# Pooled keys by transposing transfers and VectorE instead of TensorE, from the third batch on

## The chip, the cores and the metric

The kernel runs on one core of a Trainium2 chip. The metric is the device time of one execution in microseconds (us), lower is better. The engines of the core run side by side and wait for one another through semaphores: TensorE (PE in the profile, its weight loads PEld), VectorE (DVE), ScalarE (ACT), GpSimd (POOL) and SyncE (SP), which here only issues transfers.

## The reference

Attention with pooled keys and values (8 batches, 8 heads, 576 tokens, 64 wide), then a token-mixing and channel-mixing block on x of 8 batches, 576 tokens, 512 wide:

```python
def _attn_ref(q, k, v):
    k_p = k.reshape(B, H, 72, 8, D).mean(axis=3)
    v_p = v.reshape(B, H, 72, 8, D).mean(axis=3)
    scores = scale * np.matmul(q, k_p.transpose(0, 1, 3, 2))
    scores = scores - np.max(scores, axis=-1, keepdims=True)
    attn = np.exp(scores)
    attn = attn / (np.sum(attn, axis=-1, keepdims=True) + 1e-09)
    return np.matmul(attn, v_p)

def _moe_ref(x, alpha1, beta1, w_tok, alpha2, beta2, w_ch1, w_ch2, lam):
    a1 = alpha1 * x + beta1
    tok = np.einsum('ts,bsd->btd', w_tok, a1)
    u = x + lam * tok
    a2 = alpha2 * u + beta2
    ch = np.maximum(a2 @ w_ch1, 0.0) @ w_ch2
    return u + lam * ch
```

So every eight neighbouring tokens of k give one pooled key, and each query is compared with 72 of them.

## The kernel before

The work runs in nine blocks of 512 tokens (block n has four chunks of 128 tokens). Beside the MLP of block n (mlp_A, then mlp_B or from block 2 on the seven products of product, with their sums in hidden_sum and gather) the kernel does the attention and token mixing of batch b = n + 1. Block 0 does batch 1; batch 0 comes ahead of the loop. The order on every engine is written by hand: each block makes a list of (time, step) pairs, sorts it by the times (numbers of about 0 to 32, not microseconds) and calls the steps in that order. An engine executes its instructions in the order of these calls, and SP and GpSimd issue their transfers in that order too. Steps near 29 of one block and near 0 of the next are neighbours.

k of a batch is handled in two halves u of four heads. load_k reads four tokens of each head per partition in float32. sum_k, on GpSimd, adds the four tokens, and writes the sum twice, side by side, in bfloat16 (k_bf, 128 partitions x 4 heads x 2 x 64; L373 and L375). att_K, on TensorE, makes pooled, transposed keys of it: for each head one matmul with k_bf as stationary operand and pool_main as moving one (L633; pool_main holds 0.125 where two partitions belong to one pooled token, 64 columns), and two more matmuls for the last 64 tokens of the heads (L639, from rem_k with pool_rem). The result ps_kp (128 x 288) goes from PSUM to kp_pool[u] by a cast (L645; VectorE, for batch 2 ScalarE). The last tokens ("rem", 512 to 575) of q and k are loaded by load_rem, and cast and added by cast_rem on GpSimd; for batches from 3 on a one-element memset of VectorE ahead of it (behind) sets when it may begin. att_Frem turns the q part by a transposing transfer on SP (L609), att_F turns q itself (L585), mix_uT turns the mixed tokens u_bf (L849).

att_S4(b, u) makes the scores: matmuls of kp with qT (L701) and with rem_qT (L708), and exp on ScalarE (L730) follows. att_V pools v on VectorE in three steps (L671), att_AV multiplies (L744, L748) and VectorE scales the result (L750, L752). load_v sends v of the next batch from SP; its buffer is free when att_V has read it. load_q_bf sends q from GpSimd, with a cast from float32 to bfloat16.

The listed times that matter: in the blocks of batches 3 to 7 sum_k stands at -0.9 and 0.3, load_q_bf of the next batch at 0.4 and 0.5, the first half of att_V at 0.2, 1.4 and 2.2, load_v of the next batch at 3.5 and 7.5, att_K at 4.1 and 6.1, hidden_sum 3 at 4.6, the second half of att_V from 5.0, att_S4 at 6.3 and 13.6. The stores of the block before stand at its 27.2 and 29.2, after att_Frem (26.72). In batch 2's block att_K stands at 2.9 and 4.9; its sum_k is done a block ahead.

wt_bf holds w_tok until it is transposed at the start; weight_sum later takes its place for T1, a sum of weights.

Of the kernel before, what the change touches and what calls it, by code (L numbers as in the profile page):

```python
# [7 lines left out]
FP = mybir.dt.float32  # L8
F16 = mybir.dt.float16
BF = mybir.dt.bfloat16  # L10
AF = mybir.ActivationFunctionType
ALU = mybir.AluOpType
AX = mybir.AxisListType

P = 128
# [195 lines left out]
def kernel(  # L211
# [18 lines left out]
    nc = tc.nc  # L230
    fast = ctx.enter_context(ExitStack())
    fast.enter_context(tc.manual_schedule())
    B, H, S, D = q.shape

    const = fast.enter_context(tc.tile_pool(name="const", bufs=1))
    work = fast.enter_context(tc.tile_pool(name="work", bufs=1))
# [16 lines left out]
    st1 = {}  # L253
# [97 lines left out]

    def cast_rem(b, eng, copy=None, behind=None):
        raw = st1[b]["rem_raw"]
        rq = work.tile([P, 2, 2, D], BF, tag="rem_q", bufs=2, name="rem_q")
        if behind is not None:
            behind.memset(rq[:, 0, 0, 0:1], 0.0)
        rk = work.tile([P, 2, 2 if b else 3, D], BF, tag="rem_k", bufs=2, name="rem_k")
        (copy or eng.tensor_copy)(out=rq.rearrange("p c h d -> p h c d"), in_=raw[:, 0])
        twice = [raw[:, 1, :, c].unsqueeze(2).to_broadcast((P, 2, 2, D)) for c in range(2)]
        if b:  # L360
            eng.tensor_tensor(out=rk, in0=twice[0], in1=twice[1], op=ALU.add)
        st1[b]["rem"] = rq, rk

    def cast_rem_k(eng):
        raw, rk = st1[0]["rem_raw"], st1[0]["rem"][1]
        eng.tensor_copy(out=rk[:, :, 0:2], in_=raw[:, 1])
        eng.tensor_copy(out=rk[:, :, 2], in_=raw[:, 1, :, 0])
# [11 lines left out]
    wt_bf = const.tile([P, 5 * S + 64], BF, tag="wt_bf", name="wt_bf")  # L379
# [65 lines left out]
    vp1_pool, kpT_pool, kp_pool, ET_pool = [], [], [], []  # L445
    for i in range(4):
        if i < 2:
            t = const.tile([SPG, 4, 66], F16, tag=f"vp1_{i}", name=f"vp1_{i}")
            nc.vector.memset(t, 8.0)
            vp1_pool.append(t)  # L450
            t = const.tile([P, 2, 4, SPG], BF, tag=f"kpT_{i}", name=f"kpT_{i}")
# [3 lines left out]
    for i in range(2):  # L455
        t = const.tile([SPG, 4, S + 64], F16, tag=f"ET_{i}", name=f"ET_{i}")
# [147 lines left out]
    def att_Frem(b, copy=None):  # L604

        st = st1[b]
        st["rem_qT"] = work.tile([P, 2, P], BF, tag="rem_qT", bufs=2, name="rem_qT")
        if copy is None:
            nc.sync.dma_start_transpose(out=st["rem_qT"],  # L609
                                        in_=st["rem"][0].rearrange("p c h d -> p (c h d)"))  # L610
            return
        ps_q = gp("ps_qr").bitcast(BF)
        for c in range(2):
            nc.tensor.transpose(out=ps_q[:, 128 * c:128 * c + 128],
                                in_=st["rem"][0][:, c].rearrange("p h d -> p (h d)"),
                                identity=identity_bf)
        copy(out=st["rem_qT"], in_=ps_q[:, 0:256].rearrange("p (c t) -> p c t", c=2))

    def double_k(u):

        nc.vector.tensor_copy(out=st1[0]["k"][u][:, :, 4], in_=st1[0]["k"][u][:, :, 0])
        if u == 0:
            cast_rem_k(nc.vector)

    def att_K(b, u, copy):

# [63 lines left out]
    def att_S4(b, u):  # L690

        st = st1[b]
        qT, kp, rest = st["qT"][u], kp_pool[u], st["rem_qT"]
        lo = [psB.tile([P, DM], FP, tag="ch", bufs=2, name="ps_s") for _ in range(2)]
        hi = [gp("ps_s") for _ in range(2)]
        r = [gp("ps_r")[0:SPG, 0:128].rearrange("p (h i) -> p h i", i=64) for _ in range(2)]

        def main(i):
            for a in range(2):
                rows = slice(64 * a, 64 * a + 64)  # L700
                nc.tensor.matmul(  # L701
                    out=(hi if i > 1 else lo)[a][0:SPG, 256 * (i % 2):256 * (i % 2) + 256],
                    lhsT=kp[rows, i, :], rhs=qT[rows, 2 * i:2 * i + 2, :])

        def rests(i):
            for a in range(2):
                rows = slice(64 * a, 64 * a + 64)
                nc.tensor.matmul(  # L708
                    out=r[a][:, i // 2], lhsT=kp[rows, i + a, :],
                    rhs=rest[rows, :, 2 * u + i // 2::4].rearrange("p c i -> p i c"))  # L710

        pairs = ((lo, 0), (hi, 2)) if u else ((hi, 2), (lo, 0))
        main(pairs[0][1])
        rests(pairs[0][1])
        main(pairs[0][1] + 1)
        main(pairs[1][1])
        rests(pairs[1][1])
        main(pairs[1][1] + 1)
        ET = ET_pool[u]
        for i in range(4):  # L720
            st["ET"][4 * u + i] = ET[:, i]

        def exp(k):
            if k < 2:
                o, i = ET[:, k::2, 512:S], r[k]
            else:
                a, (pair, h) = k % 2, pairs[k // 2 - 1]
                o = ET[:, h:h + 2, 256 * a:256 * a + 256]
                i = pair[a][0:SPG, :].rearrange("p (h i) -> p h i", i=256)
            nc.scalar.activation(out=o, in_=i, func=AF.Exp, bias=0.0, scale=0.125)  # L730

        st["exp", u] = exp

# [40 lines left out]

    def good_sums():

        lo = work.tile([P, H * B * 5], FP, tag="u_bf", bufs=4, name="good")
        hi = work.tile([P, H * B * 5], FP, tag="u_bf", bufs=4, name="good")
        every = recs.rearrange("p h b c -> p (h b c)")
        g = nc.gpsimd  # L780
        g.tensor_scalar(out=lo, in0=every, scalar1=MIN_REC, scalar2=None, op0=ALU.is_gt)
        g.tensor_scalar(out=hi, in0=every, scalar1=MAX_REC, scalar2=None, op0=ALU.is_lt)
        g.tensor_tensor(out=lo, in0=lo, in1=hi, op=ALU.mult)
        n = H * B * 5
        while n % 2 == 0:
            n //= 2
            g.tensor_tensor(out=lo[:, 0:n], in0=lo[:, 0:n], in1=lo[:, n:2 * n], op=ALU.add)
        for i in range(1, n):
            g.tensor_tensor(out=lo[:, 0:1], in0=lo[:, 0:1], in1=lo[:, i:i + 1], op=ALU.add)
        line = work.tile([1, P], FP, tag="u_bf", bufs=4, name="good_line")  # L790
        g.dma_start(out=line, in_=lo[:, 0:1])
        n = P
        while n > 1:
            n //= 2
            g.tensor_tensor(out=line[:, 0:n], in0=line[:, 0:n], in1=line[:, n:2 * n], op=ALU.add)
        g.tensor_scalar(out=flag, in0=line[:, 0:1], scalar1=P * H * B * 5 - 0.5, scalar2=None,
                        op0=ALU.is_lt)
# [127 lines left out]
    HALF = DM // 2  # L925
    wino = {}
# [4 lines left out]
    def weight_sum(i, g):  # L931
        lo, hi = w2[g], w2[g + 2]
        if not wino:
            wino["T1"] = const.tile([P, 8, HALF], BF, tag="wt_bf", name="w2_t1")
            both = const.tile([P, 6 * DM], BF, tag="vecs", name="w2_t3")
            wino["T3"] = both[:, 0:2048].rearrange("p (j d) -> p j d", d=HALF)
            spare = both[:, 2048:3072].rearrange("p (j t) -> p j t", t=HALF)
            wino["T2"] = [work.tile([P, 4, HALF], BF, tag="q_bf", bufs=4, name="w2_t2")
                          for _ in range(2)]
            wino["S2"] = [const.tile([P, 4, HALF], BF, tag=tag, name="h_s")  # L940
                          for tag in ("early", "al2_bc")]
            wino["S3"] = [const.tile([P, 4, HALF], BF, tag="lam_bc", name="h_s"), spare]
        T1, T2, T3, T4 = (wino["T1"][:, 4 * g:4 * g + 4], wino["T2"][g],
                          wino["T3"][:, 4 * g:4 * g + 4], lo[:, :, HALF:])
        o, a, b = {
            1: (T1, lo[:, :, HALF:], lo[:, :, 0:HALF]),
            3: (T3, hi[:, :, HALF:], lo[:, :, HALF:]),
            2: (T2, hi[:, :, HALF:], T1),
            4: (T4, hi[:, :, 0:HALF], T2),
        }[i]  # L950
        nc.vector.tensor_tensor(out=o, in0=a, in1=b, op=ALU.subtract)
# [150 lines left out]
    def attention(b):  # L1102


        first = b == 1
# [15 lines left out]
        for u in range(2):  # L1121
            if b != 2:
                todo.append((3.6 + 0.1 * u if first else -0.9 + 1.2 * u,
                             lambda u=u: sum_k(b, u, nc.gpsimd)))
            if first:
                todo.append((19.1 + 0.1 * u, lambda u=u: sum_k(2, u, nc.gpsimd)))
            todo.append((7.0 + 2.3 * u if first else (2.9 if b == 2 else 4.1) + 2.0 * u,
                         lambda u=u: att_K(b, u, nc.scalar.copy if b == 2 else nc.vector.tensor_copy)))
        for u in range(2):
            at = (9.0 if first else 6.3, 13.6)[u]  # L1130
            todo.append((at, lambda u=u: att_S4(b, u)))
# [144 lines left out]
```

## Time and profile before

| | us |
|---|---|
| three runs | 334.39, 339.01, 338.86 |
| their median | 338.86 |
| the profiled execution | 334.72 |
| span in its profile | 333.2 |

The profile is of one execution, and its numbers are to be held against 334.72. The span is cut into 40 equal slices in its second part; each digit is the busy share of an engine in tenths, the DMA row that of the core's 16 DMA engines:

```profile
## 2 busy tenths in 40 slices
PE   7999999999999999999999999999999999999994
...
DVE  6773376999579969776967797878687783363263
...
PEclk9999999999999999999999999999999999999999
DMA  7999979965894982499449933994340034003003
```

The clock granted to TensorE is full everywhere. The DMA row has a rhythm of one block (about 34 us, four slices): one or two full slices, then quieter ones.

In the rows of time that follow, the first number is the start in us from the beginning of the span, the second the duration; then come the engine, the line of the kernel, the operation, out<-in by the program's names, shapes, the count of merged instructions, and in brackets the idle time ahead with what ended it. For SP the duration is that of issuing. When a transfer has landed is told by completion events: each transfer raises a semaphore, and the last increment of it marks the landing.

### The profile page before, as it was taken

What the parts mean: (1) busy time and instruction counts of PE and PEld (TensorE: products, weight loads), DVE (VectorE), ACT (ScalarE), POOL (GpSimd) and SP (SyncE); (2) the same over time, 40 slices, a digit from 0 to 9 for tenths busy, and PEclk for the clock granted to TensorE, in tenths of its full rate; (3) what the DMA queues carried; (4) which work ended last, traced back from release to release, by engine and by line L of the source; (5) the groups of instructions that cost most, each with busy time, mean ns of one, the idle gap of its engine ahead of it and who ended that gap; (6) DMA issues with size and microseconds to landing.
All of it is one profiled execution on the core that took longest, in us unless ns stands there. A gap on an engine that the chain in (4) does not pass through costs nothing.

```text
span 333.2 us, 6535 instructions
## 1 busy us (share of the span) xinstructions
PE 325.3 (98%) x2524; PEld 209.2 (63%) x2524; DVE 233.1 (70%) x473; ACT 176.1 (53%) x324; POOL 117.8 (35%) x142
## 2 busy tenths in 40 slices
PE   7999999999999999999999999999999999999994
PEld 2667754455444576656775677557755765586583
DVE  6773376999579969776967797878687783363263
ACT  3776999368422861388128802781278235704700
POOL 8769535996247010800280027102610225100000
PEclk9999999999999999999999999999999999999999
DMA  7999979965894982499449933994340034003003
GB/s 113 197 205 278 280 153 268 161 175 124 169 264 69 226 175 80 91 233 164 138 120 215 173 117 90 218 184 151 65 136 2 0 65 143 4 0 128 0 31 96
DMA packets 66203, 45.83 MB, mean 138 GB/s; under 512 B 34381, under 2 KB 56533, under 8 KB 66170
## 3 DMA queue, kind: packets, MB, share of 16 engines
q1 hardware_dynamic: 51788, 32.60, 40.9%
q0 software_dynamic: 13856, 12.40, 22.2%
q10 hardware_dynamic: 526, 0.40, 0.5%
q8 instruction: 20, 0.33, 0.4%
q14 instruction: 13, 0.11, 0.1%
HBM read 38.30 MB, written 9.44 MB: 143 GB/s over the span
## 4 chain that ended last, share of the span: by engine, by line
PE 92%; DVE 4%; DMA 2%; issue 1%; ACT 0%; DVEq 0%; POOLq 0%
PE ps_h L878 35%; PE ps_w L994 26%; PE ps_tok L830 12%; PE ps_ch L898 8%; PE ps_av L744 2%; PE ps_s L701 2%; DVE v_u L671 2%; DMA q_bf<-in_q_dram 2%; PE ps_kp L633 1%; PE ps_q L590 1%; DVE x_tm L752 1%; PE ps_r L708 1%; PE ps_av L748 1%; PE ps_sc L681 0%; PE ps_warm L821 0%
## 5 line engine op out<-in xcount | busy, mean ns | idle before, releaser
L878 PE MATMUL ps_h<-u_fm,w 128*128 128x512 bf16 (+2 forms) x608 | 133.9, 369 | 0.8 <-DVE x_tm L752 0.3
L885 ACT ACTIVATE H<-ps_h,bias_cols 128x512 bf16<-128x512 f32 x144 | 98.2, 688 | 56.5 <-PE ps_h L878 55.4
L878 PEld LDWEIGHTS <-w 128*128 128x128 bf16 x608 | 65.7, 114 | 50.3 <-issue 2.6
L994 PEld LDWEIGHTS <-H 128*128 128x128 bf16 x560 | 53.5, 98 | 10.8 <-DVE u_sb L1012 1.2
L838 ACT CAST u_bf<-u_sb 128x512 bf16<-128x512 f32 x32 | 19.8, 619 | 70.6 <-issue 41.2
L994 PE MATMUL ps_w<-w,H 128*128 128x256 bf16 x448 | 53.8, 273 | 0.0
L766 POOL TENSOR_TENSOR xs<-x_tm,lamal_bc 128x512 bf16<-128x512 f32 x12 | 15.2, 1267 | 107.2 <-DVE x_tm L752 107.0
L1012 DVE TENSOR_TENSOR u_sb<-u_sb,ps_w 128x512 f32<-128x512 f32 x54 | 36.4, 685 | 18.7 <-PE ps_w L994 18.2
L830 PE MATMUL ps_tok<-xs,wtT 128*128 128x512 bf16 (+3 forms) x200 | 44.9, 380 | 0.0
L834 DVE TENSOR_TENSOR u_sb<-x_tm,ps_tok 128x512 f32<-128x512 f32 (+1 forms) x40 | 27.4, 684 | 10.4 <-PE ps_tok L830 10.4
L752 DVE TENSOR_TENSOR x_tm<-ps_av,recs 128x320 f32<-128x320 f32 x64 | 31.5, 491 | 2.7
L730 ACT ACTIVATE ET<-ps_s 72x512 f16<-72x512 f32 x56 | 32.3, 592 | 0.0
L898 PE MATMUL ps_ch<-w,H 128*128 128x512 bf16 x128 | 30.4, 379 | 0.0
L830 PEld LDWEIGHTS <-wtT 128*128 128x128 bf16 (+3 forms) x200 | 17.4, 100 | 16.0 <-issue 1.1
L671 DVE TENSOR_TENSOR v_u<-v_u 72x1024 f32<-72x1024 f32 (+1 forms) x24 | 25.3, 1053 | 0.2
L750 DVE RECIPROCAL recs<-ps_av 128x5 f32<-128x5 f32 x64 | 12.1, 189 | 18.1 <-PE ps_av L748 17.7
L994 PE MATMUL ps_w<-w_t,h_s 128*128 128x256 bf16 x168 | 22.6, 272 | 0.0
L898 PEld LDWEIGHTS <-H 128*128 128x128 bf16 x128 | 12.0, 98 | 13.7 <-issue 0.4
L373 POOL TENSOR_TENSOR k_raw<-k_raw 128x512 f32<-128x512 f32 x14 | 18.7, 1337 | 3.1 <-DMA k_raw<-in_k_dram 3.1
L963 DVE TENSOR_TENSOR H<-H,H 128x1024 bf16<-128x1024 bf16 x14 | 9.7, 690 | 14.3 <-ACT H L885 14.2
L375 POOL TENSOR_TENSOR k_bf<-k_raw 128x512 bf16<-128x512 f32 x14 | 19.1, 1367 | 1.1
L994 PEld LDWEIGHTS <-h_s 128*128 128x128 bf16 x168 | 16.4, 98 | 4.1
(158 smaller groups left out, 370.5 us busy)
## 6 DMA issues: line engine op xcount, KB each, us to landing
out_dram<-u_sb SPq DMA_DIRECT2D x30, 256.0 KB
k_raw<-in_k_dram SPq DMA_DIRECT2D x12, 512.0 KB
v_u<-in_v_dram SPq DMA_DIRECT2D x12, 512.0 KB
q_bf<-in_q_dram POOLq DMA_DIRECT2D x16, 256.0 KB, 6.2
w<-in_moe_w_ch_dram POOLq DMA_DIRECT2D x6, 512.0 KB, 12.9
out_dram<-u_sb SPq DMA_DIRECT2D x10, 128.0 KB
w<-in_moe_w_ch_dram POOLq DMA_DIRECT2D x1, 1024.0 KB, 15.0
k_raw<-in_k_dram POOLq DMA_DIRECT2D x2, 512.0 KB, 16.9
```

Of the source, the lines that this page charges most:

```text
L375: eng.tensor_tensor(out=bf, in0=twice[0], in1=twice[1], op=ALU.add)
L671: nc.vector.tensor_tensor(out=out, in0=t[:, :, 0:width], in1=t[:, :, width:2 * width], op=ALU.add)
L730: nc.scalar.activation(out=o, in_=i, func=AF.Exp, bias=0.0, scale=0.125)
L752: nc.vector.tensor_tensor(out=x[:, 1 - odd:6 - odd, dd:dd + D], in0=av[:, :, 0:64], in1=rec.unsqueeze(2).to_broadcast((P, 5, D)), op=ALU.mult)
L830: nc.tensor.matmul(out=ps_tok[p0:p1], lhsT=wtT[0:kk, at, P * c:P * c + p1 - p0], rhs=xs_pool[i][0:kk, sc, :], start=(sc == 0), stop=(sc == 4))
L834: nc.vector.tensor_tensor(out=s["u"][p0:p1, :], in0=x[p0:p1, 1 + c if c < 4 else 5 - 5 * i, :], in1=ps_tok[p0:p1, 0:DM], op=ALU.add)
L838: nc.scalar.copy(out=s["u_bf"], in_=s["u"])
L878: nc.tensor.matmul(out=ps_h[:, t0:t1 + one], lhsT=w1_of(cc, j), rhs=rhs, start=(cc == 0), stop=(cc == 3))
L885: nc.scalar.activation(out=H4[n, j // 4][:, j % 4, :], in_=ps_h, func=AF.Relu, bias=bias_cols[:, j:j + 1], scale=1.0)
L898: nc.tensor.matmul(out=ps, lhsT=H_of(n, j)[:, 128 * m:128 * m + 128], rhs=w2[j // 4][:, j % 4, :], start=(j == 0), stop=(j == NJ - 1))
L994: nc.tensor.matmul(out=ps, lhsT=stat(j), rhs=moving(j), stop=(j == 7), start=(first and (pp == 0 or alone) and j == 0), skip_group_check=True)
L1012: nc.vector.tensor_tensor(out=o, in0=o, in1=banks[key, "both"], op=ALU.add)
```

## The change

For batches 2 to 7 att_K is no longer called. Two new steps take its place. turn_k sends k_bf of a half (128 x 512) through a transposing transfer on SP into a tile kT; there is one such tile for each half. pool_k, on VectorE, adds neighbouring columns of kT into kp_pool (the two partitions that the matmul summed are neighbouring columns now). For the last tokens cast_rem writes q and k side by side in one tile of 512 columns, att_Frem turns both in one transfer into late["rem"], and pool_k(b, 0) sums k's part, four by four, in two reductions for both halves, from which pool_k(b, 0) and pool_k(b, 1) copy their share. The factor 0.125 that pool_main held moves into the scale of the exponential. For batch 2 turn_k is listed at 28.3 of the block before, ahead of the transposes of q, and pool_k at 0.1 of its own; for later batches turn_k at 0.35 and 0.95, pool_k at 4.1 and 6.1. Four tiles change place: late["rem"] and T1 share one tile in wt_bf's place, and the tiles of good_sums take places of rem_raw and k_bf instead of u_bf.

```diff
--- before.py
+++ after.py
@@ -351,15 +351,21 @@
 
     def cast_rem(b, eng, copy=None, behind=None):
         raw = st1[b]["rem_raw"]
-        rq = work.tile([P, 2, 2, D], BF, tag="rem_q", bufs=2, name="rem_q")
+        if b > 1:
+            both = work.tile([P, 4, 2, D], BF, tag="rem_k", bufs=2, name="rem_qk")
+            rq, rk = both[:, 0:2], both[:, 2:4]
+        else:
+            rq = work.tile([P, 2, 2, D], BF, tag="rem_q", bufs=2, name="rem_q")
+            rk = work.tile([P, 2, 2 if b else 3, D], BF, tag="rem_k", bufs=2, name="rem_k")
         if behind is not None:
             behind.memset(rq[:, 0, 0, 0:1], 0.0)
-        rk = work.tile([P, 2, 2 if b else 3, D], BF, tag="rem_k", bufs=2, name="rem_k")
         (copy or eng.tensor_copy)(out=rq.rearrange("p c h d -> p h c d"), in_=raw[:, 0])
         twice = [raw[:, 1, :, c].unsqueeze(2).to_broadcast((P, 2, 2, D)) for c in range(2)]
         if b:
             eng.tensor_tensor(out=rk, in0=twice[0], in1=twice[1], op=ALU.add)
         st1[b]["rem"] = rq, rk
+        if b > 1:
+            st1[b]["rem_both"] = both
 
     def cast_rem_k(eng):
         raw, rk = st1[0]["rem_raw"], st1[0]["rem"][1]
@@ -604,11 +610,15 @@
     def att_Frem(b, copy=None):
 
         st = st1[b]
+        if copy is None:
+            if not late:
+                late["room"] = const.tile([P, 2560], BF, tag="wt_bf", name="late_room")
+                late["rem"] = late["room"][:, 2048:2560].rearrange("p (c t) -> p c t", c=4)
+            st["rem_qT"] = late["rem"][:, 0:2]
+            nc.sync.dma_start_transpose(out=late["rem"],
+                                        in_=st["rem_both"].rearrange("p c h d -> p (c h d)"))
+            return
         st["rem_qT"] = work.tile([P, 2, P], BF, tag="rem_qT", bufs=2, name="rem_qT")
-        if copy is None:
-            nc.sync.dma_start_transpose(out=st["rem_qT"],
-                                        in_=st["rem"][0].rearrange("p c h d -> p (c h d)"))
-            return
         ps_q = gp("ps_qr").bitcast(BF)
         for c in range(2):
             nc.tensor.transpose(out=ps_q[:, 128 * c:128 * c + 128],
@@ -621,6 +631,29 @@
         nc.vector.tensor_copy(out=st1[0]["k"][u][:, :, 4], in_=st1[0]["k"][u][:, :, 0])
         if u == 0:
             cast_rem_k(nc.vector)
+
+    late = {}
+    rest_sums = const.tile([P, 2, 4, 8], FP, tag="rest_sums", name="rest_sums")
+
+    def turn_k(b, u):
+
+        if ("k", u) not in late:
+            late["k", u] = const.tile([P, 4, P], BF, tag=f"kpT_{u}", name="kT")
+        nc.sync.dma_start_transpose(out=late["k", u],
+                                    in_=st1[b]["k"][u].rearrange("p h a d -> p (h a d)"))
+
+    def pool_k(b, u):
+
+        kT = late["k", u].rearrange("p h (g r) -> p h g r", r=2)
+        nc.vector.tensor_tensor(out=kp_pool[u][:, :, 0:64], in0=kT[:, :, :, 0], in1=kT[:, :, :, 1],
+                                op=ALU.add)
+        for hh in range(0 if u else 2):
+            nc.vector.tensor_reduce(
+                out=rest_sums[:, hh], op=ALU.add, axis=AX.X,
+                in_=late["rem"][:, 2 + hh].rearrange("p (g i a) -> p a g i", i=4, a=4))
+        nc.vector.tensor_copy(
+            out=kp_pool[u].rearrange("p (r h) g -> p h r g", h=2)[:, :, :, 64:72],
+            in_=rest_sums[:, :, 2 * u:2 * u + 2])
 
     def att_K(b, u, copy):
 
@@ -727,7 +760,8 @@
                 a, (pair, h) = k % 2, pairs[k // 2 - 1]
                 o = ET[:, h:h + 2, 256 * a:256 * a + 256]
                 i = pair[a][0:SPG, :].rearrange("p (h i) -> p h i", i=256)
-            nc.scalar.activation(out=o, in_=i, func=AF.Exp, bias=0.0, scale=0.125)
+            nc.scalar.activation(out=o, in_=i, func=AF.Exp, bias=0.0,
+                                 scale=0.125 if b < 2 else 0.125 * 0.125)
 
         st["exp", u] = exp
 
@@ -774,8 +808,8 @@
 
     def good_sums():
 
-        lo = work.tile([P, H * B * 5], FP, tag="u_bf", bufs=4, name="good")
-        hi = work.tile([P, H * B * 5], FP, tag="u_bf", bufs=4, name="good")
+        lo = work.tile([P, H * B * 5], FP, tag="rem_raw", bufs=2, name="good")
+        hi = work.tile([P, H * B * 5], FP, tag="rem_raw", bufs=2, name="good")
         every = recs.rearrange("p h b c -> p (h b c)")
         g = nc.gpsimd
         g.tensor_scalar(out=lo, in0=every, scalar1=MIN_REC, scalar2=None, op0=ALU.is_gt)
@@ -787,7 +821,7 @@
             g.tensor_tensor(out=lo[:, 0:n], in0=lo[:, 0:n], in1=lo[:, n:2 * n], op=ALU.add)
         for i in range(1, n):
             g.tensor_tensor(out=lo[:, 0:1], in0=lo[:, 0:1], in1=lo[:, i:i + 1], op=ALU.add)
-        line = work.tile([1, P], FP, tag="u_bf", bufs=4, name="good_line")
+        line = work.tile([1, P], FP, tag="k_bf", bufs=2, name="good_line")
         g.dma_start(out=line, in_=lo[:, 0:1])
         n = P
         while n > 1:
@@ -931,7 +965,7 @@
     def weight_sum(i, g):
         lo, hi = w2[g], w2[g + 2]
         if not wino:
-            wino["T1"] = const.tile([P, 8, HALF], BF, tag="wt_bf", name="w2_t1")
+            wino["T1"] = late["room"][:, 0:2048].rearrange("p (j d) -> p j d", d=HALF)
             both = const.tile([P, 6 * DM], BF, tag="vecs", name="w2_t3")
             wino["T3"] = both[:, 0:2048].rearrange("p (j d) -> p j d", d=HALF)
             spare = both[:, 2048:3072].rearrange("p (j t) -> p j t", t=HALF)
@@ -1124,8 +1158,13 @@
                              lambda u=u: sum_k(b, u, nc.gpsimd)))
             if first:
                 todo.append((19.1 + 0.1 * u, lambda u=u: sum_k(2, u, nc.gpsimd)))
-            todo.append((7.0 + 2.3 * u if first else (2.9 if b == 2 else 4.1) + 2.0 * u,
-                         lambda u=u: att_K(b, u, nc.scalar.copy if b == 2 else nc.vector.tensor_copy)))
+            if first:
+                todo.append((28.3 + 0.01 * u, lambda u=u: turn_k(2, u)))
+                todo.append((7.0 + 2.3 * u, lambda u=u: att_K(b, u, nc.vector.tensor_copy)))
+                continue
+            if b > 2:
+                todo.append((0.35 + 0.6 * u, lambda u=u: turn_k(b, u)))
+            todo.append((0.1 + 0.01 * u if b == 2 else 4.1 + 2.0 * u, lambda u=u: pool_k(b, u)))
         for u in range(2):
             at = (9.0 if first else 6.3, 13.6)[u]
             todo.append((at, lambda u=u: att_S4(b, u)))
```

## The prediction

> **What bounds the kernel now.** First the page: busy time, then the chain of work that ended last.
>
> ```profile
> PE 325.3 (98%) x2524; PEld 209.2 (63%) x2524; DVE 233.1 (70%) x473; ACT 176.1 (53%) x324; POOL 117.8 (35%) x142
> ...
> PE 92%; DVE 4%; DMA 2%; issue 1%; ACT 0%; DVEq 0%; POOLq 0%
> ```
>
> TensorE is busy for 325.3 of 333.2 us. Whatever makes it wait in the middle is added to the end; whatever leaves it is taken off. Start and end aside, the chain leaves PE for more than a moment only once, at 70.5 to 83.9 us (batch 2's attention), where it runs through VectorE.
>
> Then one steady block, that of batch 4 (block 3, from 139.3 us), in order of time on PE:
>
> ```profile
> 143.61 0.28 PE L633 MATMUL ps_kp<-pool_main,k_bf 128*128 128x64 bf16 x4
> 143.73 0.21 PE L639 MATMUL ps_kp<-pool_rem,rem_k 128*128 128x16 bf16 x2
> 143.78 1.90 PE L878 MATMUL ps_h<-u_fm,w 128*128 128x512 bf16 x8
> 145.52 0.28 PE L633 MATMUL ps_kp<-pool_main,k_bf 128*128 128x64 bf16 x4
> 145.63 0.20 PE L639 MATMUL ps_kp<-pool_rem,rem_k 128*128 128x16 bf16 x2
> 145.77 0.30 PE L701 MATMUL ps_s<-qT,kp 64*72 64x256 bf16 x2
> ```
>
> Durations overlap in the pipeline, so I count from start to start: six k matmuls hold PE for 143.78 - 143.61 = 0.17 us. The scores (L701) follow the second six directly: k must be ready by 145.77.
>
> The same stretch on SP's queue, through which every transposing transfer goes:
>
> ```profile
> 139.10 0.58 SPq L921 DMA_DIRECT2D out_dram<-u_sb  x1
> 139.73 0.58 SPq L917 DMA_DIRECT2D out_dram<-u_sb  x1
> 140.41 1.31 SPq L849 DMA_TRANSPOSE u_fm<-u_bf  x1
> 141.82 1.00 SPq L917 DMA_DIRECT2D out_dram<-u_sb  x2
> 143.12 5.69 SPq L348 DMA_DIRECT2D v_u<-in_v_dram  x4
> ```
>
> SP issues stores, a transpose, stores, then v. The durations are those of issuing alone. Last the DMA share, in a quiet stretch and in this one:
>
> ```profile
> 130.50:138.00 7.50, 7.50 (x60) 5.00 (x58) 6.09 (x12) 2.65 (x5) 4.79 (x5) 1.00 0.34 70
> 139.30:149.00 9.70, 9.70 (x66) 5.48 (x64) 7.79 (x12) 7.16 (x13) 1.57 (x3) 1.00 1.09 211
> ```
>
> The last two columns are DMA share and GB/s: 0.34 of the sixteen engines against all of them. At the block's start q_bf loads (GpSimd issues two at 139.32 and 140.12) and stores of the block before fill the engines. The trace's completion events (the last increment of each transfer's semaphore) show what that does to SP's queue. In the quiet stretch transposes of 128x512 land 2.4 us after their issue begins. In the busy one: store of 139.73 at 144.02, transpose of 140.41 at 147.54, stores of 141.82 and 142.41 at 148.07 and 148.81. They land in the order of issue, and the transpose's packets begin at 144.0, when the store ahead is through. So SP's queue is served in order, and a transpose waits for every store ahead.
>
> **The change part by part.** The profiled execution took 334.72 us; sums stand against that. The median is 338.86 (runs 334.39, 339.01, 338.86), so the profile is like the fastest run, and 1.2% under the median.
>
> *Removed from PE:* twelve matmuls for each of batches 2 to 7, two groups of 0.17 us: 0.34 x 6 = 2.0 us off the path.
>
> *VectorE:* pool_k(b,0) is one add, two reductions and a copy, pool_k(b,1) an add and a copy. None is in the trace. The add (128x256, bf16) is nearest to the last v sum, 0.42 us (72x256); the reduction has the same shape as L468, 0.27; the copy of 128x32 lies between a memset (0.06) and the reciprocal of 128x5 (0.18), I take 0.18. So pool_k(b,0) is 0.42 + 2 x 0.27 + 0.18 = 1.1 us and pool_k(b,1) 0.6, less two casts of 0.45 from batch 3 on (batch 2's were ScalarE's): +0.8 a block. From batch 3 on VectorE is busy 5.4 of the first 6.5 us of most blocks, so those 0.8 are hidden; only batch 2 pays.
>
> *SP's queue and the new wait.* turn_k(b,0) and (b,1) stand behind the previous block's last stores and ahead of v. Each holds SP for 1.2 to 1.3 us (the u_fm rows); v of batch b+1 goes out 2.5 us later, and is wanted a block later: nothing. GpSimd has k_bf ready (139.37 for batch 4) before SP comes to it (142.8). Now pool_k(b,0) makes VectorE wait for the landing. Behind it on VectorE stand a hidden sum (L963) and the second half of v's sums, and PE's scores wait for kp, with everything behind them. The stores ahead are unchanged, so turn_k lands after them. Its own packets take 0.6 us of all sixteen engines in the quiet stretch (512 packets of 256 bytes); beside q_bf loads the u_fm transposes took 2.2 and 3.5 us after the store ahead landed (batches 6 and 4). I take 0.6 where q_bf is through (or, in batch 3, nearly), 2.2 for batch 5, whose second q_bf lands at 184.10. kp is ready 1.1 us after that, and the loss is against the start of the scores in the profile, which holds the 0.34 already:
>
> - batch 3: last store 113.11, kT 113.7, kp 114.8, scores were at 110.85: +3.9
> - batch 4: 148.81, 149.4, 150.5; 145.77: +4.7
> - batch 5: 180.64, 182.8, 183.9; 179.39: +4.5
> - batch 6: 217.32, 217.9, 219.0; 214.30: +4.7
> - batch 7 (no q_bf loads beside it): 247.31, 247.9, 249.0; 247.92: +1.1
>
> *Batch 2* has no such crowd: its turn_k goes out behind the transpose of 68.41, from 69.7 and 71.0, and lands after 2.4 us, at 72.1 and 73.4. VectorE comes to pool_k at 71.9, so pool_k(2,0) ends at 73.2 and pool_k(2,1) at 74.0, and v's sums begin 2.2 us later than now (71.81). That is the stretch where PE already waits for VectorE: +2.2, with its 0.34 inside. qT lands at 75.1 instead of 72.45 and makes the scores 0.8 late (74.34), inside these 2.2.
>
> *The rest:* q and k's last tokens in one transfer add 256 columns to one with slack (rem_qT lands at 139.26, used at 145.90). The scale of the exponential is a constant. good_sums' tiles end a wait of GpSimd (L781, 9.6 us) on which nothing hangs. Nothing.
>
> Sum: 2.2 + 3.9 + 4.7 + 4.5 + 4.7 + 1.1 = 21.1; 334.72 + 21.1 = 355.8, say 356.
>
> Bounds: pool_k(b,0) at 0.7 (short copy, overlapped starts), turn_k at 0.6 everywhere, batch 2 at 1.5: 1.5 + 3.5 + 4.3 + 2.5 + 4.3 + 0.7 = 16.8. The other end: pool_k at 1.9, as VectorE's v sums beside GpSimd ran near twice as long (72x512: 1.36 against 0.68), turn_k at 2.2 in batch 3 and 3.5 in batch 5: 3.2 + 6.3 + 5.5 + 6.6 + 5.5 + 1.9 = 29.0.
>
> The Trainium skill, VectorE: DVE Perf Modes, "The three transpose paths", speaks against such a change: it lists 390 ns for a bf16 block of 128x128 on TensorE and 1309 ns by DMA. By an estimate from that page four blocks one after another would take 5.2 us, 2.8 more than the quiet row, and the sum 17 us more. The trace disagrees: four blocks land in 2.4 us from issue.
>
> **The rivals.** (A) *The transfers land in time.* If a transpose were not held by the stores ahead, it would land 2.4 us after issue. With issue right behind the stores (106.7, 142.9, 175.3, 211.7, 244.5) kp would come at 110.6 (VectorE is free for it at 109.5), 146.4, 178.8, 215.2, 248.0: against the scores -0.3 (the removed matmuls alone), +0.6, -0.3, +0.9, +0.1, and +2.2 for batch 2: +3, 338. With batch 2 covered too, only PE's 2.0 us are left: 332.7, faster than before. It decides where landing follows issue by less than about 2 us more than in the quiet stretch. For it: the quiet rows, 130 to 138 us. Against: the 7.1 us of the transpose of 140.41, one place ahead in the same queue. The Trainium skill, DMA: Bandwidth & Descriptors, "Rules for kernel authors", gives this rival as a rule: issue early, wait late, and the fixed setup cost is overlapped. The quiet transposes agree with it; the one of 140.41 does not.
>
> (B) *Part of it.* Landings are receipts, and packets of the next transfer may run before them; if turn_k came 2 us sooner each time, the stalls were 1.9 + 2.7 + 2.5 + 2.7 + 0, with batch 2 +12: 347.
>
> (C) *VectorE becomes the bound everywhere:* +0.8 in five blocks, +2.2, -1.7 for the matmuls of those five: +4.5, 339. Against: its idle time ahead of kp's cast is 0.9 us in the blocks of batches 4 to 7.
>
> **How the numbers follow.** Two per cent, 6.8 us, is about what a measurement of this kernel can tell from no change. Forecast 0.70, B 0.10 (both slower by over 2%), A 0.13 and C 0.03 (within), and 0.04 for a gain of over 2%, which the 2.0 us of PE can't give except through the spread of the runs. So 0.80, 0.16, 0.04. The range runs from below B to the upper bound on the scale of the median: (334.72 + 29.0) x 338.86 / 334.72 = 368; low 343 leaves out A and C.
>
> **What would show it.** In the changed profile: no L633 or L639 rows after 36 us; PE idle of 3 to 5 us ahead of the first scores of batches 3 to 6, released by VectorE; VectorE idle ahead of pool_k's add, released by the DMA of kT; kT landing behind the stores ahead of it. Wrong if kT lands within 3 us of issue in those blocks, or VectorE does not wait there; then A holds.

## The result and the profile after

The changed kernel takes 365.46 us (median of 4 runs, 363.39 to 366.04) against 338.91 (median of 4, 334.39 to 339.01): ratio 1.0813, 95% interval 1.0727 to 1.0898. It is slower, by more than the sum of the prediction but inside its range. The profiled execution took 365.94 us against 334.72, 31.2 us more.

The page of the changed kernel, first its busy times, then clock and DMA in 40 slices, then the chain that ended last by engine:

```profile
PE 330.6 (91%) x2421; PEld 210.2 (58%) x2452; DVE 237.7 (65%) x499; ACT 176.2 (48%) x322; POOL 117.2 (32%) x142
...
PEclk9999999999999899989999799989999999999999
DMA  8999949768889671798439691697435005203002
...
PE 74%; DMA 11%; DVE 9%; issue 2%; SPq 2%; POOL 0%; DVEq 0%; POOLq 0%
```

PE's share of the chain fell from 92 to 74%, and DMA and VectorE took over. The clock row, flat before, has four dips. Who waited for whom, over the whole span (us in total, times, longest):

```profile
DVE kp L648 <- DMA kT<-k_bf: 27.2, 6, 7.1
...
PE ps_s L734 <- DVE kp L654: 21.7, 5, 5.7
```

That is the wait of the prediction: VectorE waits for kT in all six batches, and PE waits for VectorE's kp ahead of five groups of scores. Batch 4's block again, SP's queue, then VectorE, then PE. The block starts 10.4 us later than before the change (149.7 instead of 139.3), so add that when comparing:

```profile
150.81 1.31 SPq L883 DMA_TRANSPOSE u_fm<-u_bf  x1
152.21 1.00 SPq L951 DMA_DIRECT2D out_dram<-u_sb  x2
153.31 4.00 SPq L642 DMA_TRANSPOSE kT<-k_bf  x2
```

```profile
153.05 0.42 DVE L704 TENSOR_TENSOR vp<-v_u 72x256 f16<-72x256 f32 x1
160.16 0.42 DVE L648 TENSOR_TENSOR kp<-kT 128x256 bf16<-128x256 bf16 x1 [6.68 <-DMA kT<-k_bf]
160.50 0.47 DVE L651 TENSOR_REDUCE rest_sums<-late_room 128x32 f32<-128x128 bf16 x2
161.00 0.18 DVE L654 CAST kp<-rest_sums 128x32 bf16<-128x32 f32 x1
```

```profile
149.68 6.21 PE L912 MATMUL ps_h<-u_fm,w 128*128 128x512 bf16 x27
161.24 0.43 PE L734 MATMUL ps_s<-qT,kp 64*72 64x256 bf16 x2 [5.36 <-DVE kp L654]
161.46 0.28 PE L741 MATMUL ps_r<-late_room,kp 64*72 64x64 bf16 x2
...
162.39 3.53 PE L912 MATMUL ps_h<-u_fm,w 128*128 128x512 bf16 x11
```

By the completion events the two stores issued at 152.21 and 152.79 land at 158.82 and 159.95, and kT, issued at 153.31, at 160.13: right behind them. VectorE takes it up at 160.16, kp is done at 161.18, PE starts at 161.24. The last row holds something the prediction did not have: eleven matmuls of 512 columns in 3.53 us, where twelve took 2.78 at the same place before the change:

```profile
146.48 2.78 PE L878 MATMUL ps_h<-u_fm,w 128*128 128x512 bf16 x12
```

Stretches of the changed kernel's execution (the column before the last two is the granted clock):

```profile
156.00:161.00 5.00, 0.00 (x0) 0.00 (x0) 0.81 (x3) 0.61 (x1) 0.00 (x0) 1.00 1.15 247
161.00:164.40 3.40, 3.16 (x17) 1.58 (x18) 3.35 (x7) 1.00 (x4) 0.00 (x0) 0.50 0.44 84
164.40:168.00 3.60, 3.55 (x25) 1.99 (x25) 2.75 (x7) 3.60 (x7) 0.00 (x0) 1.00 0.55 129
```

PE stands still for 5 us, and then works at half clock for 3.4. The trace's clock records show four such times in the middle: 3.41 us from 120.03, 3.41 from 160.99, 6.83 from 198.53, 3.41 from 242.91. The first begins 0.4 us after the stall of batch 3 has ended (119.65), the others within the stalls of batches 4, 5 and 6.

### The profile page after: what moved, and what is told of

The parts are those of the page before. It is cut to its first block, busy times and chain, and to the rows that moved or that the text cites. A ratio compares the mean times of both kernels' runs of the same rounds, so it can differ in the third digit from the quotient of the medians.

```text
span 364.0 us, 6390 instructions
## 1 busy us (share of the span) xinstructions
PE 330.6 (91%) x2421; PEld 210.2 (58%) x2452; DVE 237.7 (65%) x499; ACT 176.2 (48%) x322; POOL 117.2 (32%) x142
## 4 chain that ended last, share of the span: by engine, by line
PE 74%; DMA 11%; DVE 9%; issue 2%; SPq 2%; POOL 0%; DVEq 0%; POOLq 0%
PE ps_h L912 24%; PE ps_w L1028 24%; PE ps_tok L864 10%; DMA kT<-k_bf 10%; PE ps_ch L932 6%; PE ps_av L778 2%; PE ps_s L734 2%; DVE v_u L704 2%; DMA q_bf<-in_q_dram 1%; SPq L951 1%; DVE kp L648 1%; DVE w L963 1%; DVE u_sb L868 1%; DVE u_sb L1046 1%; PE ps_q L596 1%
## 5 line engine op out<-in xcount | busy, mean ns | idle before, releaser
L912 PEld LDWEIGHTS <-w 128*128 128x128 bf16 x608 | 66.7, 115 | 57.2 <-issue 10.1
L800 POOL TENSOR_TENSOR xs<-x_tm,lamal_bc 128x512 bf16<-128x512 f32 x12 | 15.2, 1268 | 133.6 <-DVE x_tm L786 133.4
L864 PE MATMUL ps_tok<-xs,wtT 128*128 128x512 bf16 (+2 forms) x193 | 44.5, 380 | 0.4
L734 PE MATMUL ps_s<-qT,kp 64*72 64x256 bf16 x112 | 12.9, 308 | 22.3 <-DVE kp L654 21.7
L864 PEld LDWEIGHTS <-wtT 128*128 128x128 bf16 (+3 forms) x200 | 17.4, 100 | 16.0 <-issue 1.1
L704 DVE TENSOR_TENSOR v_u<-v_u 72x1024 f32<-72x1024 f32 (+1 forms) x24 | 23.6, 984 | 0.2
L648 DVE TENSOR_TENSOR kp<-kT 128x256 bf16<-128x256 bf16 x12 | 5.8, 483 | 27.2 <-DMA kT<-k_bf 27.2
L734 PEld LDWEIGHTS <-kp 64*72 64x72 bf16 x112 | 6.7, 122 | 28.6 <-DVE kp L654 24.9
```

The costliest lines, as they stand in the source:

```text
L704: nc.vector.tensor_tensor(out=out, in0=t[:, :, 0:width], in1=t[:, :, width:2 * width], op=ALU.add)
L734: nc.tensor.matmul(out=(hi if i > 1 else lo)[a][0:SPG, 256 * (i % 2):256 * (i % 2) + 256], lhsT=kp[rows, i, :], rhs=qT[rows, 2 * i:2 * i + ...
L864: nc.tensor.matmul(out=ps_tok[p0:p1], lhsT=wtT[0:kk, at, P * c:P * c + p1 - p0], rhs=xs_pool[i][0:kk, sc, :], start=(sc == 0), stop=(sc == 4))
L912: nc.tensor.matmul(out=ps_h[:, t0:t1 + one], lhsT=w1_of(cc, j), rhs=rhs, start=(cc == 0), stop=(cc == 3))
```

## The experiments

Times of single executions differ by up to 3.8 us before any changed step runs (the last section has the numbers). So one number is given for all beside the time: the stretch from the first token-mixing matmul (L830 before, L864 after) to the last matmul, both by their starts in the trace. It is 328.33 - 21.60 = 306.7 us before the change and 358.93 - 24.11 = 334.8 in the changed kernel. Four single executions ran first, beside one of 335.54 of the kernel before on the same chip.

**Stores behind turn_k.** Only the order in SP's queue:

```diff
-        store(n, m)
+        if n == 0 or m < 2:
+            store(n, m)
...
-                for m in range(4):
+                for m in range(4 if n > 5 else 0):
...
+        if 2 <= n <= 6:
+            for m in range(2 if n == 2 else 0, 4):
+                todo.append((1.2 + 0.01 * m, lambda m=m: store(n - 1, m)))
```

> Only the order on SP's queue changes: in the blocks of batches 3 to 7 the stores of the block before (for batch 3 the last two of them) go out behind turn_k, not ahead. GpSimd's q_bf loads stay as they are. Theory (turn_k waits in its queue for the stores ahead of it): kT lands before VectorE comes to it in batches 3, 5 and 7, and at most 2 us late in batches 4 and 6, where one u_fm transpose stays ahead of it; the stalls of 4.4, 5.1, 5.5, 5.1 us ahead of the scores shrink to under 1 us in batches 3 and 5 and under 2.5 us in 4 and 6, the half clock after them goes, and the time is 336 to 343 us. Rival (a transpose is slow whenever q_bf loads run beside it, whatever stands ahead of it): the stalls stay over 3 us in batches 4 and 6, time over 352. Rival (VectorE's new work is what is late): nothing changes, 360 to 367.

Measured: 343.82 us, stretch 311.5. The waits, the same two rows:

```profile
DVE kp L648 <- DMA kT<-k_bf: 8.6, 4, 3.5
...
PE ps_s L734 <- DVE kp L654: 3.6, 2, 2.1
```

23 of the 28 us of the stretch are back. kT(3, 0), (5, 0) and (7, 0) land 2.4 to 2.5 us after issue. The new order does two things for them: no store is ahead any more, and (3, 0) and (5, 0) go out 1.6 and 1.0 us ahead of the first q_bf load (batch 7 has none). (4, 0) and (6, 0) go out 0.3 and 0.6 us behind that load, and land 7.0 and 5.9 us after issue. Only a u_fm transpose stands ahead of them, and it has landed at 146.07 and 217.26, 5.8 and 4.8 us before kT does. kT(5, 1) has nothing but kT(5, 0) ahead, and lands 5.7 us behind it. So a transpose beside q_bf loads is slow with no store ahead of it: in this the first rival was right. Its stalls of over 3 us did not come because turn_k now goes out 3.4 and 3.2 us earlier in these two blocks, counted from the token-mixing matmuls before them. Two stalls are left, the longest 2.1 us, and the clock stays full through them. The time is 0.8 us above the range expected because this execution's start took 3.8 us longer than that of the kernel before.

**q_bf loads out of the way.** The queue's order is the changed kernel's; the loads beside it go out later:

```diff
-                    at = {1: 14.0, 2: 6.5}.get(b, 0.4) + 0.1 * u
+                    at = {1: 14.0, 2: 6.5}.get(b, 6.2) + 0.01 * u
...
-                        b + 1, u, nc.vector if b == 2 else None)))
+                        b + 1, u, nc.vector if b >= 2 else None)))
```

> Only the q_bf loads move: in the blocks of batches 3 to 6 they wait for a memset of VectorE that stands behind pool_k, so they no longer run beside the stores and turn_k. The queue order on SP is that of the changed kernel. Theory (stores that share the DMA engines with q_bf loads are slow, and the queue passes their delay on to turn_k): the stores ahead land within 3 us of their issue, turn_k within 3.5 us, stalls under 1.5 us, time 337 to 344 us. Rival (the order in the queue alone, whatever the load): stalls over 3 us and 352 or more. Rival (VectorE's new work): 360 to 367.

Measured: 338.81 us, stretch 310.0.

```profile
DVE kp L648 <- DMA kT<-k_bf: 8.4, 5, 2.5
...
PE ps_s L734 <- DVE kp L654: 2.8, 3, 1.2
```

Now kT lands 2.4 to 2.6 us after issue for batches 3 to 6, though the same stores stand ahead of it, and the longest stall is 1.2 us. From issue to landing, in us, by completion events (in brackets how long after the first q_bf load kT was issued):

| | changed kernel | stores behind | q_bf out of the way |
|---|---|---|---|
| kT(3, 0) | 7.4 (2.2) | 2.5 (-1.6) | 2.5 |
| kT(4, 0) | 6.8 (3.6) | 7.0 (0.3) | 2.6 |
| kT(5, 0) | 8.4 (1.1) | 2.4 (-1.0) | 2.6 |
| kT(6, 0) | 6.7 (3.8) | 5.9 (0.6) | 2.6 |
| kT(7, 0), no q_bf load | 3.2 | 2.4 | 3.2 |

So the q_bf load is what makes kT late: without it the order costs 0.8 us at most (batch 7), and beside it kT is late with stores ahead or without. In the changed kernel the delay falls on the stores ahead, and the queue hands it on. The order counts because it decides whether turn_k goes out before the loads begin. How long kT would take at its place in the changed kernel, beside the loads but without the stores, was not tried. Either change removes over four fifths of the loss.

**PE kept busy in the stall.** Twenty matmuls with an unused result ahead of the scores:

```diff
+        if not u and 2 < b < 7:
+            busy = psB.tile([P, DM], FP, tag="ch", bufs=2, name="ps_busy")
+            for _ in range(20):
+                nc.tensor.matmul(out=busy, lhsT=w2[3][:, 0, 0:P], rhs=w2[3][:, 0])
```

> The changed kernel with twenty matmuls of 128x512 (about 4.3 us) whose result nobody uses ahead of the first scores of batches 3 to 6, so that PE waits at most about 1 us there. Theory (after the stalls PE runs at a granted clock of 0.5 for one or two periods of 3.41 us, which costs 1.3 to 1.6 us in each of four blocks): the granted clock stays 1.0 from the start-up to the tail, the scores begin when they did, and the time falls by 5 to 6.5 us to 357 to 361. Rival (the blocks lose that time because VectorE has a backlog after its wait): the time stays at 363 to 367.

Measured: 359.06 us, stretch 330.3; the clock records show no half clock between 10.47 us and the tail. Batch 4's block on PE:

```profile
151.47 4.48 PE L729 MATMUL ps_busy<-w 128*128 128x512 bf16 x20
158.88 0.30 PE L738 MATMUL ps_s<-qT,kp 64*72 64x256 bf16 x2 [2.92 <-DVE kp L654]
...
159.59 2.78 PE L916 MATMUL ps_h<-u_fm,w 128*128 128x512 bf16 x12
```

PE still waits, for 2.92 us, and the twelve matmuls behind take 2.78 us as before the change. The stretch fell by 4.5 us, not 5 to 6.5; 2.3 us of the fall in time are a shorter start. But the part that the clock owns can be read without the rest: from the first scores of a batch to the first token-mixing matmul of its block it is 15.83 us in all four batches before the change, 17.42, 17.22, 17.46 and 17.11 in the changed kernel, and 15.83 four times here. The half clock costs 1.59 + 1.39 + 1.63 + 1.28 = 5.9 us, and all of it goes. VectorE's backlog behind its wait, the rival, costs nothing that this shows. The missing 1.4 us lie ahead of the scores, which begin 1.9 and 0.6 us later in the blocks of batches 4 and 6 than in the changed kernel, and 0.4 and 0.8 earlier in those of 3 and 5: batch 4's kT lands 8.7 us after issue here, 6.8 there.

**Nobody waits.** kT and k's turned last tokens are sent and not read; the keys come from the old matmuls:

```diff
-                                 scale=0.125 if b < 2 else 0.125 * 0.125)
+                                 scale=0.125)
...
-            todo.append((0.1 + 0.01 * u if b == 2 else 4.1 + 2.0 * u, lambda u=u: pool_k(b, u)))
+            todo.append(((2.9 if b == 2 else 4.1) + 2.0 * u, lambda u=u: att_K(
+                b, u, nc.scalar.copy if b == 2 else nc.vector.tensor_copy)))
```

> The transfers of the changed kernel all go out (turn_k, the joint one of q and k), but kT and k's turned last tokens are never read: the pooled keys of batches 2 to 7 come from the matmuls of the kernel before, at their old places, with the old scale. Theory (the wait is what costs, not the traffic): 334 to 341 us, and no idle time of PE ahead of the scores in batches 3 to 7. Rival (twelve more transposes on SP's queue crowd out v, k, u_fm and the stores): 345 or more.

Measured: 336.85 us, stretch 306.8, that of the kernel before (306.7). kT lands late as in the changed kernel (7.8 us after issue in batches 4 and 5, 6.5 and 5.4 in 3 and 6), and PE goes on without a gap:

```profile
147.35 0.28 PE L666 MATMUL ps_kp<-pool_main,k_bf 128*128 128x64 bf16 x4
147.47 0.20 PE L672 MATMUL ps_kp<-pool_rem,rem_qk 128*128 128x16 bf16 x2
147.60 0.30 PE L734 MATMUL ps_s<-qT,kp 64*72 64x256 bf16 x2
```

The transfers, the joint one of q and k among them, cost nothing. The whole cost is with the reader: VectorE's wait for kT, and pool_k itself, which this run leaves out too. The next two runs part these.

**turn_k ahead of the stores, and the same with batch 2 left to TensorE.** Both were timed against the kernel before in five rounds. The first moves turn_k to the end of the block before:

```diff
-            if b != 2:
-                todo.append((3.6 + 0.1 * u if first else -0.9 + 1.2 * u,
-                             lambda u=u: sum_k(b, u, nc.gpsimd)))
+            if first:
+                todo.append((3.6 + 0.1 * u, lambda u=u: sum_k(b, u, nc.gpsimd)))
+            elif b < B - 1:
+                todo.append((23.2 + 0.1 * u, lambda u=u: sum_k(b + 1, u, nc.gpsimd)))
+                todo.append((27.0 + 0.01 * u, lambda u=u: turn_k(b + 1, u)))
...
-            if b > 2:
-                todo.append((0.35 + 0.6 * u, lambda u=u: turn_k(b, u)))
```

> The changed kernel with turn_k of batches 3 to 7 listed at 27.0 of the block before, right behind att_Frem and ahead of the stores and of the fifth u_fm transpose (sum_k is called earlier for that, at the same place in GpSimd's order). q_bf loads as in the changed kernel. Theory (only the place in the queue and the load beside it made turn_k late): kT lands 2.4 to 4 us after issue and ahead of VectorE in all five blocks, no stall ahead of their scores; each of the five blocks is 0.3 us shorter than before the change (the matmuls gone), batch 2's block still 1.9 longer. From the first token-mixing matmul to the last matmul 307 us (306.7 before the change, 334.8 in the changed kernel), time 333 to 340 by the start-up clock, ratio 0.99 to 1.01. Rival (matmuls removed gain nothing because other work of the block fills the time): 308.5 or more for that stretch.

Measured: 335.84 us (median of 12) against 335.9 (median of 23), ratio 1.000, interval 0.996 to 1.0039; stretch 307.1. SP's queue and PE in batch 4's block:

```profile
141.65 2.53 SPq L642 DMA_TRANSPOSE kT<-k_bf  x2
144.27 1.22 SPq L955 DMA_DIRECT2D out_dram<-u_sb  x2
```

```profile
144.84 4.05 PE L912 MATMUL ps_h<-u_fm,w 128*128 128x512 bf16 x18
148.81 0.30 PE L734 MATMUL ps_s<-qT,kp 64*72 64x256 bf16 x2
```

kT(b, 0) lands 2.4 to 2.5 us after issue in all five blocks; in those of batches 3 to 6 it goes out 0.7 to 1.4 us ahead of the first q_bf load. kT(b, 1), a place behind it, takes up to 6.4 us beside the q_bf loads, again with no store ahead, but is wanted later. The scores follow the MLP's matmuls with no gap, and the five blocks are 0.30 to 0.35 us shorter than before the change, as the removed matmuls said. Batch 2's block is still 2.0 us longer. The second version takes that away:

```diff
-                                 scale=0.125 if b < 2 else 0.125 * 0.125)
+                                 scale=0.125 if b < 3 else 0.125 * 0.125)
...
-                todo.append((28.3 + 0.01 * u, lambda u=u: turn_k(2, u)))
...
-            todo.append((0.1 + 0.01 * u if b == 2 else 4.1 + 2.0 * u, lambda u=u: pool_k(b, u)))
+            if b == 2:
+                todo.append((2.9 + 2.0 * u, lambda u=u: att_K(b, u, nc.scalar.copy)))
+            else:
+                todo.append((4.1 + 2.0 * u, lambda u=u: pool_k(b, u)))
```

> As the run before it, and batch 2's pooled keys by TensorE as before the change (no turn_k and pool_k there; its scale stays 0.125). Theory (batch 2's loss of 1.9 us is VectorE's, which has no idle time in that stretch, and five blocks gain 0.34 us each): from the first token-mixing matmul to the last matmul 305.0 us, 1.7 under the kernel before the change, ratio 0.990 to 1.000. Rival (batch 2's loss lies in the order of SP's queue around its block or the joint transfer of last tokens): 306.5 or more.

Measured: 334.12 us (median of 12), ratio 0.9943, interval 0.9915 to 0.9971; stretch 305.7. This beats both kernels, by about half a per cent of the one before: the interval leaves out 1, but the gain is less than the 2% that the prediction counts as a change. The stretch is between the theory's 305.0 and the rival's 306.5. Batch 2's block is 0.46 us longer than before the change; its profile has a wait of 1.33 us there that the kernel before doesn't show:

```profile
70.81 2.75 PE L912 MATMUL ps_h<-u_fm,w 128*128 128x512 bf16 x12 [1.33 <-DMA u_fm<-u_bf]
```

That u_fm transpose stands in SP's queue behind the joint transfer of the last tokens, which waited for GpSimd. The changed kernel has the same wait (1.34 us), and the execution in which nobody waits has 0.92 us and no loss in its block. The wait is not what costs: VectorE sets the length of this block, and is behind earlier. It starts the first product ahead of v's sums (L941; L907 before) 12.72 us after the block's first token-mixing matmul here and in the changed kernel, 12.27 before the change and 12.29 where nobody waits. The last v sum ends 26.30, 27.71, 25.84 and 25.88 us into the block in the same four executions, and the length of the block moves with it. The other runs that keep pool_k are as late at L941 (12.7 to 12.8). Why VectorE is behind there stays open.

## Why the prediction was right, and where its sum was short

It forecast slower, 356 us in a range of 343 to 368, and the time is 365.46. Between the two profiles, 31.2 us apart, the parts come out so (by the starts of the first scores and of the first token-mixing matmul in each block):

| part | predicted | measured |
|---|---|---|
| batch 2's block | +2.2 | +1.9 |
| stall of batch 3 | +3.9 | +4.4 |
| batch 4 | +4.7 | +5.1 |
| batch 5 | +4.5 | +5.5 |
| batch 6 | +4.7 | +5.1 |
| batch 7 | +1.1 | +0.2 |
| half clock behind four stalls | 0 | +5.9 |
| the start, before any changed step | 0 | +2.5 |
| the tail, and what lies around the span | 0 | +0.6 |
| sum | 21.1 | 31.2 |

*The number* is in the range partly by luck. The bounds of the sum end at +29.0, 363.7 us, and the two profiles are 31.2 apart; what brings 365.46 inside is the step from the profile to the median of three runs (363.7 to 368; 23 later executions of the kernel before have a median of 335.9), and not one of the terms that were missing.

*The wait.* Right in place and direction; the stalls of batches 3 to 6 came out 0.4 to 1.0 us longer than forecast. kT landed 0.2 to 0.5 us behind the last store ahead of it in batches 3, 4, 6 and 7 (0.6 was taken), 2.7 in batch 5 beside a q_bf load (2.2). The stores themselves were taken as unchanged. The last one ahead landed 0.4 to 0.8 us later within its block than before the change in batches 3 to 6, and 0.7 earlier in batch 7, which accounts for most of the differences. That a transpose waits for every store ahead fits these landings, but is half of the cause: with the q_bf loads moved and the order kept the delay is gone, and with the stores moved and the loads kept it stays wherever kT still goes out beside a load.

*Removed matmuls.* 0.34 us for each batch, confirmed by 0.30 to 0.35 where nothing waits.

*VectorE.* pool_k(4, 0) took 1.02 us from 160.16 (1.1 predicted). Batch 2's pool_k, beside GpSimd's work, took 3.6 us instead of 1.7:

```profile
75.16 1.20 DVE L648 TENSOR_TENSOR kp<-kT 128x256 bf16<-128x256 bf16 x1 [0.29 <-DMA kT<-k_bf]
...
77.67 1.13 DVE L654 CAST kp<-rest_sums 128x32 bf16<-128x32 f32 x1
78.71 2.79 DVE L704 TENSOR_TENSOR v_u<-v_u 72x1024 f32<-72x1024 f32 x2
```

It waited for kT only 0.3 us there, and the v sums behind ran faster than before, so that the block lost 1.9 us after all, of which 0.45 lie ahead of pool_k (the last run above): the term came out, its working did not. Why the v sums ran faster was not tried.

*The term that was missing* is the clock. The sum took PE to work after a stall as it worked before it. The clock row of the profile before is flat, but its first record stands only at 9.27 us, and PE's rows ahead of it show another speed: matmuls of 128x512 start 0.43 us apart at 2.0 and 5.4 us, and 0.22 apart from 21.6 us on. Between the start and the tail of these traces, waits of PE of 4.7 us and more (4.68, 5.36, 5.74, 5.39) cost one or two periods of half clock each time; 2.9 us and less cost none. The Trainium skill, TensorE: Matmul & The Clock Gate, "Why this matters for your kernels", has the rule, no idle gaps of PE over about 3 us between bursts of matmuls, and the stalls of this case agree with it. It should have stood in the sum as 1.3 to 1.6 us for each of four stalls.

*The start* belongs to no edit. *Rivals:* A fell with the first profile, and is what the kernel becomes when turn_k is put ahead of the stores and the q_bf loads (ratio 1.000). The rule of the Trainium skill, DMA: Bandwidth & Descriptors, "Rules for kernel authors", issue early and wait late, holds there: early has to mean early in the queue, ahead of the loads. B fell with the first profile too, as kT landed behind the last store in all five blocks. C fell with the run that has turn_k ahead: with pool_k on VectorE and no wait for kT, the five blocks are 0.30 to 0.35 us shorter than before the change.

## What to carry to other kernels

Cost a transfer by what shares the DMA engines while it is under way and by what stands ahead of it in its queue, not by its own length: the same transpose landed after 2.4 us or after 8.4. Where an engine that is full is made to wait, look for what it loses after the wait as well. A step moved off the busiest engine pays only what that engine spent on it (2.0 us here), so any new wait must be shorter than that, and its place in the queue is part of the change.

## What the runs showed of the hardware that was not expected

The half clock came in pieces of 3.41 us (6.83 is two), and a piece need not lie in the stall that it follows: batch 3's began 0.4 us after its stall was over, and batch 5's two pieces began 2.5 us into its stall and ended 3.6 us after it. The price was 1.3 to 1.6 us in each block.

Executions differ at the start. The first record of a full clock and the first token-mixing matmul lie at 9.27 and 21.6 us (before the change), 10.24 and 22.1 (q_bf out of the way), 10.47 and 21.8 (PE kept busy), 14.93 and 23.4 (nobody waits), 17.63 and 24.1 (the changed kernel), 19.56 and 25.4 (stores behind): roughly, a late full clock goes with a late start. The last two kernels are full from 8.40 and 8.18 us, but have a piece of half clock from 18.64 and 18.42, and start at 23.3. No wait of PE between 8.4 and 22.2 us is longer than 0.6 us there, so a long wait was not what brought it; in the 3.4 us ahead of it PE was busy for 2.8 and 2.9 us, against 3.3 from 15.2 to 18.6 us before the change. What did bring it was not tried. Up to 3.8 us of an execution's time are settled there, about the distance between 334.39 and 339.01 of the kernel before; that those runs differ for this reason was not shown, as only one of them has a profile.
